# Sigmoid attention and an MLP mixer on one core: batch 0's u transposed by DMA, and each v loaded behind its transposed q

## The chip, the cores and the metric

The kernel runs on one core of one Trainium2 chip. The metric is the device time of one execution, in microseconds (us), on that core. The engines are named as in the profile: PE (TensorE, matrix products; PEld its weight loads), DVE (VectorE), ACT (ScalarE), POOL (GpSimd) and SP (SyncE, which here only issues DMAs). All engines run beside each other, each through its own instructions in order, and wait for one another by semaphores. DMAs are issued by SP, POOL or ACT, queue by queue, and are carried out by the core's 16 DMA engines.

## The reference

For each of 8 batches and 12 heads (448 positions, head width 64), attention with a sigmoid in place of a softmax; then, for each batch, an MLP mixer on the result x of 448 x 768.

```
scores = q @ k.T / 8 - log(448)          per head
attn   = sigmoid(scores) ;  x_head = attn @ v
x      = heads side by side              [448, 768]
h      = relu(x.T @ w_tok1) @ w_tok2     token mixing, 448 -> 256 -> 448
u      = x + h.T
out    = u + relu(u @ w_ch1) @ w_ch2     channel mixing, 768 -> 1536 -> 768
```

Inputs and output are fp32; the kernel computes in fp16 with fp32 accumulation.

## The kernel before

**Stage 1** goes through 24 units, three for each batch b: unit (b, u) holds four heads, and cycle c = 3b + u of the main loop (L566) works on it. Each unit needs q and k with the head width on the partitions ("transposed", tiles tr_q and tr_k). `qk` (L146) multiplies them in seven blocks j, and ACT takes the sigmoid (L161). `av` (L171), in the cycle behind, multiplies by v (tile raw_v) and DVE copies the result to xT (L190). x is transposed by SP's DMA (`xtrans_dma`, L200) or by PE (`xtrans`), `tok1` (L222) and `ytrans` (L249) do the token mixing, and DVE adds x to give `ut`, u with the channels on the partitions (L261).

**Stage 2** of a batch (`stage2`, L450) is the channel mixing: `ch1` (L279) in 12 column blocks of 72 products, each block copied through a relu by DVE (L294), then `ch2` (L301) for three tiles of 128 rows in two halves, and `ch2_last` (L342) for the last 64 rows. It is cut into pieces of three products, and `work` (L580) puts these between the qk blocks of the cycles after, by shares of the whole: batch 0's in cycles 4 to 7, later ones over three cycles. Batch 0 does its first halves first, since the second half of the weight c2 is loaded later (L427).

**The last addition, out = u + ...**, needs u with the positions on the partitions. Here the kernel knows two ways. From batch 1 on, `utrans` (L266) lets SP transpose the whole of `ut` by one DMA into the tile `un`, and DVE adds `un` to ch2's PSUM result (L319, L379). Where `un` does not exist, PE adds u in PSUM by products with an identity matrix (L327 for ch2, L365 for ch2_last), and DVE only copies (L334, L377). Before the change batch 0 goes the second way; so does the last tile of the last batch. Both are in the two functions:

```
    add_on_pe = final or b not in un
...
        if b in un:
            nc.vector.tensor_tensor(
                out=outs[b, t][:, cols].rearrange("s (u d) -> s u d", d=128),
                in0=un[b][:, NU * half : NU * half + NU, t, :],
                in1=ps[:, 0:DH].rearrange("s (u d) -> s u d", d=128),
                op=ADD,
            )
```

PSUM tiles of all these steps share the tag "m" with four buffers; qk's have two of their own.

**Loads and queues.** POOL issues all loads in the order of the program (`load`, L87: two DMAs, one for each half of the partitions, which also turn fp32 into fp16). Weights and batches 0 to 2 are loaded at the start. Batch 0 and some units of batches 1 and 2 are transposed by PE (`pe_transpose`, L132). The others, from batch 2's second unit on, go `through_dma` (L121): DVE regroups a unit's k or q (`relayout`, L103), and SP transposes (`dma_transpose`, L116) all units of k, then of q. These pieces are put between the pieces of stage 2 by `work`: batch 2's in cycle 5, batch 3's in cycles 7 and 8, and those of batch b + 1 from cycle 3b on.

At the end of cycle (b, 2) POOL copies two elements of the next batch's last transposed q into the tile `gate` (L632). It reads what the DMA transpose wrote, so POOL waits there, and the loads of k and q for batch b + 2 come after. The load of v for batch b + 1 stands elsewhere: in cycle (b, 0), b > 1, behind the third qk block (L599). raw_v has two buffers.

SP's queue has, in order, the transposes of x, of k and q, of u (`utrans(b - 1)` in cycle (b, 2), b > 1) and the output's stores.

Of the kernel before, what the change touches and what calls it, by code (L numbers as in the profile page):

```python
# [22 lines left out]
NU = 3  # L23
# [3 lines left out]
def kernel(  # L27
# [13 lines left out]
    B, H, S, E = q.shape  # L41
# [35 lines left out]
    def raw_tile(b, t):  # L77
        if (b, t) not in raw:
            tag, bufs = f"raw_{t}", 2 if t == "v" else 1
            if b == 1 and t != "v":  # L80
                tag = f"rel_{t}"
            raw[b, t] = pa.tile(
                [128, NU, 2, NJ, E], FP16, tag=tag, bufs=bufs, name=f"raw_{t}_{b}"
            )
        return raw[b, t]

    def load(b, t, src, u0, u1):  # L87

        for g in range(2):
            dst = raw_tile(b, t)[64 * g : 64 * g + 64, u0:u1, :, :, :]  # L90
            heads = src[b, 6 * g + 2 * u0 : 6 * g + 2 * u1]
            nc.gpsimd.dma_start(  # L92
                out=dst.rearrange("p u hi j e -> p (u hi) (j e)"),
                in_=heads.rearrange("h (p j) e -> p h (j e)", j=NJ),
            )
# [25 lines left out]
    def through_dma(b, u0):  # L121

        pieces = []
        for t in ("k", "q"):
            for u in range(u0, NU):
                pieces.append(lambda t=t, u=u: relayout(b, t, u))
            pieces.append(lambda t=t: dma_transpose(b, t, u0))
        return pieces
# [17 lines left out]
    def qk(b, u, j):  # L146
        if j == 0:
            att[b, u] = pa.tile(
                [128, 2, NJ, S], FP16, tag="att", bufs=2, name=f"att_{b}_{u}"
            )  # L150
        ps = pp.tile([128, 2, 512], FP32, tag="qk", bufs=2, name=f"qk_{b}_{u}_{j}")
        for g in range(2):
            for hi in range(2):
                nc.tensor.matmul(  # L154
                    out=ps[64 * g : 64 * g + 64, hi, 0:S],
                    lhsT=tr[b, "k"][64 * hi : 64 * hi + 64, u, j, 64 * g : 64 * g + 64],
                    rhs=tr[b, "q"][64 * hi : 64 * hi + 64, u, :, 64 * g : 64 * g + 64],
                    start=True,
                    stop=True,
                )  # L160
        nc.scalar.activation(  # L161
            out=att[b, u][:, :, j, :],
            in_=ps[:, :, 0:S],
            func=SIGMOID,
            bias=bias_t[:, :],
            scale=att_scale,
        )
# [3 lines left out]
    def av(b, u, j0=0, j1=NJ):  # L171
        if j0 == 0:
            xa[b, u] = [
                pp.tile([128, 512], FP32, tag="m", bufs=4, name=f"xa_{b}_{u}_{g}")
                for g in range(2)
            ]
        ps = xa[b, u]
        for j in range(j0, j1):
            for g in range(2):
                for hi in range(2):  # L180
                    nc.tensor.matmul(  # L181
                        out=ps[g][64 * hi : 64 * hi + 64, 0:S],
                        lhsT=raw[b, "v"][64 * g : 64 * g + 64, u, hi, j, :],
                        rhs=att[b, u][64 * g : 64 * g + 64, hi, j, :],
                        start=(j == 0),
                        stop=(j == NJ - 1),
                    )
        if j1 == NJ:
            for g in range(2):
                nc.vector.tensor_copy(  # L190
                    out=xTs[b % 2][:, u, g, 0:S], in_=ps[g][:, 0:S]
                )
# [7 lines left out]
    def xtrans_dma(b, u):  # L200
        nc.sync.dma_start_transpose(
            out=xn_tile(b)[:, u, :, :, :].rearrange("s g t d -> s (g t) d"),
            in_=xTs[b % 2][:, u, :, :].rearrange("d g s -> d (g s)"),
        )
# [61 lines left out]
    def utrans(b):  # L266
        un[b] = pa.tile([128, NDB, 4, 128], FP16, tag="un", bufs=2, name=f"un_{b}")
        nc.sync.dma_start_transpose(
            out=un[b].rearrange("s db t d -> s (db t) d"),
            in_=uts[b % 2].rearrange("d db s -> d (db s)"),  # L270
        )
# [7 lines left out]
    def ch1(b, cb, d0=0, d1=NDB):  # L279
        if cb == 0 and d0 == 0:  # L280
            h2[b] = pa.tile([128, NCB, S], FP16, tag="h2", bufs=1, name=f"h2_{b}")
        if d0 == 0:
            acc[b, cb] = pp.tile([128, 512], FP32, tag="m", bufs=4, name=f"c1_{b}_{cb}")
        ps = acc[b, cb]
        for d in range(d0, d1):
            nc.tensor.matmul(  # L286
                out=ps[:, 0:S],
                lhsT=c1[:, BY_UNIT[d], 128 * cb : 128 * cb + 128],
                rhs=uts[b % 2][:, BY_UNIT[d], 0:S],
                start=(d == 0),  # L290
                stop=(d == NDB - 1),
            )
        if d1 == NDB:
            nc.vector.tensor_scalar(  # L294
                out=h2[b][:, cb, :], in0=ps[:, 0:S], scalar1=0.0, scalar2=None, op0=MAX
            )
# [153 lines left out]
    def stage2(b):  # L450
        for cb in range(NCB):
            for d in range(0, NDB, 3):
                yield 3 * S, lambda cb=cb, d=d: ch1(b, cb, d, d + 3)
        groups = [(t, half) for t in range(3) for half in range(2)]
        if b == 0:
            groups.sort(key=lambda g: g[1])
        for t, half in groups:
            for n in range(0, NCB, 3):
                yield 3 * DH, lambda t=t, half=half, n=n: ch2(b, t, half, n, n + 3)
        for n in range(0, NCB, 3):  # L460
            yield 3 * DH, lambda n=n: ch2_last(b, n, n + 3)
# [97 lines left out]
    for cb in range(2):  # L559
        ch1(0, cb, 5, 6)  # L560

    ON_DMA = range(N_FIRST, N_CYCLES)
    ON_PE = 2 * NU + 1
    starts = [N_FIRST] + [NU * b + 5 for b in range(1, B - 1)] + [N_CYCLES + 1]
    pending, copies = [], []
    for c in range(N_FIRST, N_CYCLES + 1):  # L566
        b, u = divmod(c, NU)
        here = c < N_CYCLES
        before = divmod(c - 1, NU)
        mixed = [n for n in (c - 2, c - 1) if (n == c - 1) != (n in ON_DMA) or not here]  # L570
        if c in starts:
            lot = starts.index(c)
            first = c
            pending = list(stage2(lot))[4 if c == N_FIRST else 0 :]
            total = sum(w for w, f in pending)

            shares = [9, 9, 6, 6] if c == N_FIRST else [10, 10, 10]
            spent = [0, 0]

        def work(share):  # L580
            goal = 3 * sum(shares[: c - first]) + share * shares[c - first]
            while pending and spent[0] < total * goal / 90:
                w, f = pending.pop(0)
                f()
                spent[0] += w
                spent[1] += 1
                if copies and (c < 3 * NU or spent[1] % 2 == 0):
                    copies.pop(0)()

        if here:  # L590
            qk(b, u, 0)
            qk(b, u, 1)
        av(*before)
        if c - 1 in ON_DMA:
            xtrans_dma(*before)
        if here:
            qk(b, u, 2)
        if here and b > 1 and u == 0 and b + 1 < B:
            load(b + 1, "v", v, 0, NU)  # L599
        if c == 2 * NU + 2:  # L600
            copies += through_dma(3, 0)[NU + 1 :]
        work(1)
        if c - 1 not in ON_DMA:
            xtrans(*before)
        if c + 1 < ON_PE:
            for t in ("k", "q"):
                pe_transpose(*(divmod(c + 1, NU)[0], t, divmod(c + 1, NU)[1]))
        if here:
            qk(b, u, 3)
            qk(b, u, 4)  # L610
        if b == 1 and u == 2:
            copies = through_dma(2, 1)
        if c == 2 * NU + 1:
            copies = through_dma(3, 0)[: NU + 1]
        work(2)
        if u == 2 and b > 1:
            utrans(b - 1)
        for n in mixed:
            tok1(*divmod(n, NU))
        if here:  # L620
            qk(b, u, 5)
            qk(b, u, 6)
        if b > 2 and u == 0 and b + 1 < B:
            copies = through_dma(b + 1, 0)
        work(3)
        for n in mixed:
            ytrans(*divmod(n, NU))
        if b == 1 and u == 2:
            while copies:
                copies.pop(0)()  # L630
        if here and u == 2 and b + 2 < B:
            nc.gpsimd.tensor_copy(  # L632
                out=gate[:, :], in_=tr[b + 1, "q"][:, NU - 1, NJ - 1, 126:128]
            )
            load(b + 2, "k", k, 0, NU)
            load(b + 2, "q", q, 0, NU)
    assert not copies
    utrans(B - 1)
    for w, f in pending:
# [33 lines left out]
```

## Time and profile before

| | us |
|---|---|
| median of 3 runs | 370.6 (370.51 to 370.81) |
| the profiled execution | 370.7 |
| its span in the trace | 368.9 |
| L286, ch1's 576 products, busy | 115.5 |
| L309, ch2's 576 products, busy | 100.4 |
| L161, the 168 sigmoids, busy | 158.8 |
| L327 and L365, identity products, busy | 2.0 (18) and 0.7 (12) |
| un<-ut, 7 transposes, median to landing | 7.4 |
| raw_v, 12 whole loads of a half, median to landing | 9.8 |

A line of the profile's groups or timeline names the line of the kernel, the engine, the operation, and out<-in by the program's tile names ("c" is any tile of ch1, ch2 or their weights). The timeline gives start and duration in us; matmuls are pipelined, so neighbours overlap, and the time that one takes from PE is read from the start of the next. "To landing" runs from the issue to the semaphore of the finished DMA. In the DMA view q0 is the queue of POOL's loads and q1 that of SP's transposes and stores; a packet of a transpose is 256 bytes. In the 40 slices of the span a digit is the busy share in tenths.

### The profile page before, as it was taken

What the parts mean: (1) busy time and instruction counts of PE and PEld (TensorE: products, weight loads), DVE (VectorE), ACT (ScalarE), POOL (GpSimd) and SP (SyncE); (2) the same over time, 40 slices, a digit from 0 to 9 for tenths busy, and PEclk for the clock granted to TensorE, in tenths of its full rate; (3) what the DMA queues carried; (4) which work ended last, traced back from release to release, by engine and by line L of the source; (5) the groups of instructions that cost most, each with busy time, mean ns of one, the idle gap of its engine ahead of it and who ended that gap; (6) DMA issues with size and microseconds to landing.
All of it is one profiled execution on the core that took longest, in us unless ns stands there. A gap on an engine that the chain in (4) does not pass through costs nothing.

```text
span 368.9 us, 7559 instructions
## 1 busy us (share of the span) xinstructions
PE 361.3 (98%) x3272; PEld 196.8 (53%) x3272; DVE 181.8 (49%) x322; ACT 172.2 (47%) x212; POOL 53.0 (14%) x91
## 2 busy tenths in 40 slices
PE   8989999999999999999999999999999999999995
PEld 5545555555555555555545555555545554565553
DVE  2466657257445365364455464554552354644531
ACT  1996555665445455455445545454454554010000
POOL 8847410120030031001110030100000000000000
PEclk9999999999999999999999999999999999999999
DMA  7999999999999998769996899939910425137014
GB/s 95 176 202 190 197 205 196 140 193 226 212 171 172 204 186 156 99 129 204 177 148 85 150 188 148 170 75 176 195 22 11 112 71 110 28 78 158 2 43 107
DMA packets 103872, 51.73 MB, mean 140 GB/s; under 512 B 76000, under 2 KB 100768, under 8 KB 103840
## 3 DMA queue, kind: packets, MB, share of 16 engines
q1 hardware_dynamic: 78736, 29.47, 43.9%
q0 software_dynamic: 25024, 21.70, 39.2%
q8 instruction: 25, 0.41, 0.5%
q10 hardware_dynamic: 80, 0.10, 0.1%
q14 instruction: 7, 0.06, 0.0%
HBM read 43.38 MB, written 11.01 MB: 147 GB/s over the span
## 4 chain that ended last, share of the span: by engine, by line
PE 95%; DVE 2%; ACT 2%; issue 0%
PE c L286 30%; PE c L309 26%; PE qk L154 10%; PE xa L181 9%; PE tk L233 6%; PE yt L254 5%; PE c L354 5%; ACT att L161 2%; PE heat L469 2%; DVE xT L190 1%; PE tp_k L138 1%; PE tp_q L138 0%; DVE xn L215 0%; PE c L327 0%; DVE h L243 0%; PE xb L210 0%
## 5 line engine op out<-in xcount | busy, mean ns | idle before, releaser
L161 ACT ACTIVATE att<-qk,att_bias 128x896 f16<-128x896 f32 x168 | 158.8, 1010 | 101.7 <-PE qk L154 101.4
L286 PE MATMUL c<-ut,c 128*128 128x448 f16 x576 | 115.5, 353 | 0.0
L309 PE MATMUL c<-c,h 128*128 128x384 f16 x576 | 100.4, 326 | 0.0
L294 DVE TENSOR_SCALAR h<-c 128x448 f16<-128x448 f32 x96 | 59.8, 624 | 60.6 <-PE c L286 60.4
L286 PEld LDWEIGHTS <-c 128*128 128x128 f16 x576 | 53.3, 98 | 58.7 <-issue 13.0
L309 PEld LDWEIGHTS <-h 128*128 128x128 f16 x576 | 54.1, 98 | 42.9 <-issue 9.1
L154 PE MATMUL qk<-tr_q,tr_k 64*64 64x448 f16 x672 | 53.3, 361 | 1.1 <-ACT att L161 1.0
L319 DVE TENSOR_TENSOR o<-un,c 128x384 f32<-128x384 f16 x42 | 23.3, 554 | 62.2 <-PE c L309 62.1
L190 DVE CAST xT<-xa 128x448 f16<-128x448 f32 x48 | 27.7, 620 | 20.8 <-PE xa L181 20.8
L181 PE MATMUL xa<-att,raw_v 64*64 64x448 f16 x672 | 37.6, 350 | 0.0
L247 ACT ACTIVATE h<-tk 128x256 f16<-128x256 f32 x42 | 13.8, 380 | 49.9 <-PE tk L233 49.9
L261 DVE TENSOR_TENSOR ut<-xT,yt 128x448 f16<-128x448 f16 x48 | 27.4, 615 | 4.6 <-PE yt L254 4.4
L154 PEld LDWEIGHTS <-tr_k 64*64 64x64 f16 x672 | 15.9, 104 | 25.1 <-issue 21.7
L181 PEld LDWEIGHTS <-raw_v 64*64 64x64 f16 x672 | 22.6, 107 | 10.1 <-issue 1.3
L233 PE MATMUL tk<-xn,w 128*128 128x256 f16 x192 | 25.0, 272 | 1.3 <-DVE xn L215 0.9
L233 PEld LDWEIGHTS <-w 128*128 128x128 f16 x192 | 18.6, 98 | 7.0 <-issue 2.6
L254 PE MATMUL yt<-w,h 128*128 128x448 f16 x96 | 22.2, 353 | 0.0
L375 ACT ACTIVATE o<-c 64x384 f32<-64x384 f32 x1 | 0.5, 485 | 40.5 <-PE c L365 40.5
L632 POOL COPY gate<-tr_q 128x2 f16<-128x2 f16 x5 | 0.9, 184 | 125.2 <-DMA tr_q<-rel_q 125.2
L92 POOL DMA_DIRECT2D raw_v<-in_v_dram x20 | 13.0, 669 | 36.1 <-PE qk L154 35.9
L92 POOL DMA_DIRECT2D raw_q<-in_q_dram x26 | 16.6, 653 | 8.4 <-DMA c<-in_moe_w_ch_dram 5.0
L92 POOL DMA_DIRECT2D raw_k<-in_k_dram x26 | 16.4, 649 | 8.6 <-DMA c<-in_moe_w_ch_dram 5.2
(42 smaller groups left out, 128.4 us busy)
## 6 DMA issues: line engine op xcount, KB each, us to landing
out_dram<-o SPq DMA_DIRECT2D x48, 192.0 KB, 2.8
c<-in_moe_w_ch_dram POOLq DMA_DIRECT2D x4, 1152.0 KB, 14.3
raw_v<-in_v_dram POOLq DMA_DIRECT2D x12, 336.0 KB, 9.8
raw_k<-in_k_dram POOLq DMA_DIRECT2D x10, 336.0 KB, 6.1
raw_q<-in_q_dram POOLq DMA_DIRECT2D x10, 336.0 KB, 9.5
raw_q<-in_q_dram POOLq DMA_DIRECT2D x14, 112.0 KB, 5.6
raw_k<-in_k_dram POOLq DMA_DIRECT2D x14, 112.0 KB, 4.5
out_dram<-o SPq DMA_DIRECT2D x15, 96.0 KB, 2.3
```

What stands on the lines that cost most here:

```text
L92: nc.gpsimd.dma_start(out=dst.rearrange("p u hi j e -> p (u hi) (j e)"), in_=heads.rearrange("h (p j) e -> p h (j e)", j=NJ),)
L154: nc.tensor.matmul(out=ps[64 * g : 64 * g + 64, hi, 0:S], lhsT=tr[b, "k"][64 * hi : 64 * hi + 64, u, j, 64 * g : 64 * g + 64], rhs=tr[b, " ...
L161: nc.scalar.activation(out=att[b, u][:, :, j, :], in_=ps[:, :, 0:S], func=SIGMOID, bias=bias_t[:, :], scale=att_scale,)
L181: nc.tensor.matmul(out=ps[g][64 * hi : 64 * hi + 64, 0:S], lhsT=raw[b, "v"][64 * g : 64 * g + 64, u, hi, j, :], rhs=att[b, u][64 * g : 64 ...
L190: nc.vector.tensor_copy(out=xTs[b % 2][:, u, g, 0:S], in_=ps[g][:, 0:S])
L233: nc.tensor.matmul(out=ps[:, tcb, :, :], lhsT=w1[:, t, cols], rhs=xn[b][:, u, :, t, :], start=(t == 0), stop=(t == 3),)
L254: nc.tensor.matmul(out=ps[:, 0:S], lhsT=h1[b][:, tcb, g, u, :], rhs=w2[:, tcb, :, :], start=(tcb == 0), stop=(tcb == 1),)
L261: nc.vector.tensor_tensor(out=uts[b % 2][:, db, 0:S], in0=xTs[b % 2][:, u, g, 0:S], in1=ps[:, 0:S], op=ADD)
L286: nc.tensor.matmul(out=ps[:, 0:S], lhsT=c1[:, BY_UNIT[d], 128 * cb : 128 * cb + 128], rhs=uts[b % 2][:, BY_UNIT[d], 0:S], start=(d == 0), ...
L294: nc.vector.tensor_scalar(out=h2[b][:, cb, :], in0=ps[:, 0:S], scalar1=0.0, scalar2=None, op0=MAX)
L309: nc.tensor.matmul(out=ps[:, 0:DH], lhsT=h2[b][:, cb, 128 * t : 128 * t + 128], rhs=c2[:, cb, cols], start=(cb == 0), stop=(cb == NCB - 1 ...
L319: nc.vector.tensor_tensor(out=outs[b, t][:, cols].rearrange("s (u d) -> s u d", d=128), in0=un[b][:, NU * half : NU * half + NU, t, :], in ...
```

## The change

`utrans(0)` is called before the main loop, behind the first pieces of batch 0's ch1. So `un[0]` exists when batch 0's stage 2 is written out: its identity products are not issued, and DVE adds `un[0]` in place of its copies. And the load of v for batch b + 1 (b > 1) moves from cycle (b, 0) to the end of cycle (b, 2), behind the gate and ahead of the loads of k and q. A sixth gate is added in cycle (6, 2), for the v of batch 7. The v of batches 0 to 2 stays where it was.

```diff
     for cb in range(2):
         ch1(0, cb, 5, 6)
 
+    utrans(0)
     ON_DMA = range(N_FIRST, N_CYCLES)
...
         if here:
             qk(b, u, 2)
-        if here and b > 1 and u == 0 and b + 1 < B:
-            load(b + 1, "v", v, 0, NU)
         if c == 2 * NU + 2:
             copies += through_dma(3, 0)[NU + 1 :]
...
-        if here and u == 2 and b + 2 < B:
+        if here and u == 2 and b + 1 < B:
             nc.gpsimd.tensor_copy(
                 out=gate[:, :], in_=tr[b + 1, "q"][:, NU - 1, NJ - 1, 126:128]
             )
-            load(b + 2, "k", k, 0, NU)
-            load(b + 2, "q", q, 0, NU)
+            if b > 1:
+                load(b + 1, "v", v, 0, NU)
+            for t, src in (("k", k), ("q", q)):
+                if b + 2 < B:
+                    load(b + 2, t, src, 0, NU)
```

## The prediction

> **What bounds the kernel now.** I read the page's busy rows and the chain first, then PE's timeline around batch 0's second stage, then the DMA queues there, one microsecond at a time.
>
> ```profile
> PE 361.3 (98%) x3272; PEld 196.8 (53%) x3272; DVE 181.8 (49%) x322; ACT 172.2 (47%) x212; POOL 53.0 (14%) x91
> PE   8989999999999999999999999999999999999995
> DMA  7999999999999998769996899939910425137014
> PE 95%; DVE 2%; ACT 2%; issue 0%
> ```
>
> TensorE works for 98% of the span and is 95% of the chain. Work taken from it shortens the run; anything else counts only if PE has to wait for it. The DMA row is full up to the fifteenth slice (about 138 us), so from 38 to 138 us an added transfer delays those behind it. The clock row is 9 throughout.
>
> All working is on the profiled execution: 370.7 us, span 368.9, so 1.8 around the span. The median shown, 370.6, is 0.1 lower.
>
> **What is removed: batch 0's identity products.** PE's timeline, columns start and duration (durations overlap, so I take differences of starts):
>
> ```profile
> 62.80 0.66 PE L309 MATMUL c<-c,h 128*128 128x384 f16 x3
> 63.30 0.33 PE L327 MATMUL c<-ident,ut 128*128 128x128 f16 x3
> 63.46 2.11 PE L309 MATMUL c<-c,h 128*128 128x384 f16 x12
> ...
> 84.10 1.65 PE L354 MATMUL c<-c,h 128*64 128x384 f16 x18
> 85.59 0.33 PE L365 MATMUL c<-ident,ut 128*64 128x128 f16 x6
> 85.86 0.93 PE L254 MATMUL yt<-w,h 128*128 128x448 f16 x4
> ```
>
> Three L327 products take 63.46 - 63.30 = 0.16 us. There are six such groups (they start at 63.30, 65.41, 70.26, 73.86, 79.03 and 81.75): 0.98. The six L365 products take 85.86 - 85.59 = 0.27, of which about 0.08 stays, since batch 1's L354 group also ends 0.08 late (24 products in 2.07 us at 0.083): 0.19. Sum 1.17, call it **1.2 us saved**. The upper bound is 1.45, if the 0.26 between L327 and the next matmul of another shape (65.41 to 65.67, 81.75 to 82.01) and all 0.27 go. VectorE pays nothing: six copies of 558 ns (L334) become six adds of 554 (L319), two of 554 (L377) become two of 552 (L379).
>
> **What is added: one transpose of u, 24 blocks of 128 rows, 3072 packets of 256 B, on SP's queue.** Batch 0's last u add ends at 38.2 on DVE, and SP has issued nothing by then (its first line is at 56.91), so the issue itself delays nothing. The packets do. One-microsecond slices of the DMA queues (packets, MB, share), at 59, 61 and 70 us; q0 carries POOL's loads, q1 SP's transposes:
>
> ```profile
> q0 software_dynamic: 260, 0.20, 130.2%
> ```
> ```profile
> q0 software_dynamic: 170, 0.15, 89.2%
> q1 hardware_dynamic: 168, 0.04, 32.1%
> ```
> ```profile
> q1 hardware_dynamic: 1143, 0.28, 127.2%
> ```
>
> Alone, the loads move 260 packets per us and a transpose 1143. Together each gets about 170, packet for packet: the transpose drops to a seventh, the loads lose a quarter. (The same in 109 to 114 us: 166 to 179 each.)
>
> Now step by step. A transpose issued among loads shows its first packets 4 to 4.7 us later (56.91 to about 60.9; 103.94 to 108.6), so this one starts at 42.6. The slices from there to 67 us hold 5280 load packets, of which 3070 are of c2 (smaller: 266 per us alone, so about 185 beside a transpose). 3070 / 185 + 2210 / 172 = 29.4 us: loads that ended at about 65 to 67 now end near 72. Beside them q1 goes at about 177 per us:
> - u of batch 0: 3072 / 177 = 17.4, ends at 60, lands at 61 to 62. First needed by the add after 63.3. In time; late, it would hold PE only from about 67.4, when the four PSUM tiles "m" are used up.
> - The second half of c2 landed at 62.8 (issue 44.78 + 18.0). Its data ended at about 60.5, 17.9 us after 42.6; at the shared rate these become 25.3, so it lands at 70.2. First needed by the fourth L309 group, at 70.43 less three groups of 0.16: 69.9. **Late by 0.3.**
> - v of batch 2 landed at 66.7, now about 73.5; needed by L181 at 76.26 less 0.65. In time.
> - Behind u on SP:
>
> ```profile
> 56.91 1.34 SPq L201 DMA_TRANSPOSE xn<-xT  x1
> 62.18 4.16 SPq L116 DMA_TRANSPOSE tr_k<-rel_k  x1
> 66.39 2.99 SPq L116 DMA_TRANSPOSE tr_q<-rel_q  x1
> 69.42 1.31 SPq L201 DMA_TRANSPOSE xn<-xT  x1
> ```
>
> That is 1024 packets of xn, 1792 of tr_k, 1792 of tr_q. xn ends at 42.6 + 4096 / 177 = 65.7, lands near 67.5, needed at 71.89 - 0.5: in time. The q of batch 2 lands at 71.4 now (66.39 + 5.0). With u ahead, 7680 packets must pass. About 5000 have passed by 72; 2680 at 1143 take 2.3 us; the last packet to landing took 0.9: 75.2. SP's issue is held too: un<-ut (L268) took 8.9 us to issue at 177.97, with about 1600 packets outstanding at its end, so tr_q can't be issued freely: 75.5. Its user:
>
> ```profile
> 75.86 0.57 PE L154 MATMUL qk<-tr_q,tr_k 64*64 64x448 f16 x8
> ```
>
> This qk comes at 75.86 - 0.65 (four groups gone) = 75.2. **Late by 0.3**, the same 0.3 as c2's, not another: PE that waited for c2 comes here 0.3 later. I cost the transpose at **+0.3 us**. The ends: at 190 of each per us and a start at 42.1, q lands at 72.4 and costs 0; at 160, below any slice, loads end at 75.6, q lands at 78.6 and costs 3.4.
>
> [...]
>
> What comes after is later as well, but covered. The gate on POOL waits for that q (71.45, now near 76), so k of batch 3 lands at about 83 in place of 78.8, and its regrouping on DVE (79.87, then about 79.0) waits some 3.5 us. Behind it on DVE are the adds at 82.12 and 85.97, whose PSUM tiles PE needs again only at 86 to 87; DVE catches up in the 1.6 and 2.2 us that it idles there. Without that cover up to 2 us would come through.
>
> **What is moved: each v from batch 3 on.** v of batch 3 leaves 75.0, where it ran beside tr_k (issued 83.92 for 7.46 us, landing 10.9), so the next q transpose and its gate come earlier: DVE's regrouping ends at 91.9, hence the gate at about 96 to 98 in place of 100.12. POOL there:
>
> ```profile
> 100.12 0.18 POOL L632 COPY gate<-tr_q 128x2 f16<-128x2 f16 x1 [23.75 <-DMA tr_q<-rel_q]
> 100.72 1.32 POOL L92 DMA_DIRECT2D raw_k<-in_k_dram  x2 [0.41 <-issue]
> 102.96 1.33 POOL L92 DMA_DIRECT2D raw_q<-in_q_dram  x2 [0.92 <-issue]
> 104.26 1.34 POOL L92 DMA_DIRECT2D raw_v<-in_v_dram  x2
> ```
>
> k lands at 107.5 and 109.3, q at 111.6 and 113.8, v at 116.2 and 117.6. In the new order v takes k's place, and lands at about 109 if the gate stays, 105 if it comes early; the first L181 of batch 3 is at 115.79 - 1.2 = 114.6. Covered by 5 us or more. k takes q's place: 113.8, or about 109.5 with the early gate; its regrouping (L103) is at 110.63 - 1.2 = 109.4. DVE's next add waits 2.35 us for PE now, which takes up most of a delay. I cost it at 0; without the cover, up to 2.
>
> The other batches have more room. The gates open at 130.3, 173.1 and 216.1, and a new one for batch 7 at 252.95 + 6.7 = 259.7; add 9 to 14 for v's landing; the first L181 is at 158.4, 201.1, 243.7 and 286.4: 12 us or more each. Queued on POOL behind each gate are v, k and q only, and k and q, some 5 us later, are first used some 20 us after their gate. The u transposes issued there (133.95, 177.97, 219.30) now share with six loads in place of four, 3 to 4 us longer; the tightest, 219.30, landed 14.9 later at 234.2, now about 238, for an add at 238.05 - 1.2, and the four PSUM tiles cover about 4 us of that. Zero.
>
> **Sum:** 370.7 - 1.2 + 0.3 = 369.8 on the profiled execution, 0.1 less on the median: **369.7 us**, 0.24% faster. 0.2% (0.74 us) is about the least that a measurement of this kernel can tell from no change.
>
> **The rivals.**
> 1. *The gain is given back* (c2's second half, or batch 2's transposed q, 0.5 to 1.9 us late at 69.9 or 75.2). For it: both come out within 0.3 us of their need, and my estimates of landings are good to about 1 us. Against: u's transpose starts among loads of large packets and may go more slowly, and the loads then lose less. One us of stall gives 370.5.
> 2. *Slower: the q of batch 2 becomes the bound.* The place is the qk at 75.2; the mechanism is SP's queue, where 3072 packets now stand before xn, tr_k and tr_q, and q1 gets a seventh of its speed until the loads are out. It decides from a landing 1.9 us late, that is at 77.1 or later. By the bound of 160 packets it lands at 78.6: 370.6 - 1.2 + 3.4 = 372.8. For it: the tail after the loads is slow now too (296 to 548 q1 packets per us from 65 to 68). Against: xn between u and tr_k has long passed by then, and POOL issues no load until the q has landed, so at the end q1 is alone.
> 3. *v or k behind the gate is late.* v would have to land after 114.6, 14 us after a gate at 100; behind k and q it took 12.7 at most (issue 104.9), so only a gate later than about 101 brings it there. For it: the delay of rival 2 pushes the whole of batch 3's chain. Against: the chain loses v's 768 packets, 3.3 us of load time, ahead of it. A k or v that costs 2 us beyond its cover gives 369.7 + 2 = 371.7.
> 4. *No stall at all*, the bound of 190: 370.6 - 1.2 = 369.4, at most 1.45 saved, 369.15.
>
> **How the numbers follow.** The forecast and rival 4, at most 0.45 us of stall: 0.46 (0.20 of it rival 4). Rival 1: 0.27. Rival 2: 0.20. Rival 3: 0.07. Faster by over 0.2% means below 369.86: the first two, 0.46. Within 0.2%, up to 371.34: rival 1, 0.27. Slower: rivals 2 and 3, 0.27. The range goes from rival 4 with a little of the larger saving (369.2) to near the bound of rival 2 (372.4), so that most of both signs is in; some 0.15 is left out. The forecast's own range is 369.2 to 369.9.
>
> **What would show it.** L327 and batch 0's L365 are gone, and L319 has 48 adds. The new un<-ut is issued at 38.3, takes over 10 us to issue, and lands at 60 to 63. In 43 to 60 us q1 shows some 170 to 185 packets per us, the loads 0.13 to 0.15 MB. PE runs 0.5 us ahead at the fourth L309 group, then meets a wait of some 0.3 us on c2 or on tr_q at 75. After 87 it is ahead by a constant 0.9 and has no new waits up to the end. The second L632 starts at 96 to 98, and v lands before L181 asks for it. I am wrong if the lead grows or shrinks after 90, if L319 of batch 0 is held by un, or if q1 gets another share beside the loads than one packet for one.

## The result, and the profile after

The changed kernel takes **375.03 us** (median of 6 runs, 373.78 to 376.13); the kernel before took 370.89 on the same chip (6 runs, 370.51 to 372.0). The ratio is 1.0105, with a 95% interval of 1.0085 to 1.0125: about 1.1% slower, where 0.24% faster was forecast. The time lies above the upper end of the range, 372.4. The profiled execution took 375.4 us, with a span of 373.6: 4.7 longer than before's 368.9.

The page of the changed kernel: busy row of the engines, 40 slices of PE, of its granted clock and of the DMA engines, the chain, and the group of ch2's products.

```profile
PE 361.0 (97%) x3248; PEld 194.8 (52%) x3248; DVE 181.8 (49%) x322; ACT 172.6 (46%) x212; POOL 53.3 (14%) x92
...
PE   7989999799999999999999999999999999999995
...
PEclk9999999899999999999999999999999999999999
DMA  7999999999999899939996799919961426127014
...
PE 72%; DMA 20%; POOL 4%; DVE 2%; issue 1%; DVEq 0%; POOLq 0%
...
L309 PE MATMUL c<-c,h 128*128 128x384 f16 x576 | 101.3, 329 | 2.6 <-DMA c<-in_moe_w_ch_dram 2.6
```

PE has 24 instructions fewer (3248 against 3272), as the change intends, but its busy time hardly fell. Both the PE row and the clock row dip in the eighth slice, 65 to 75 us, and 20% of the chain now goes through a DMA. The L309 group's idle time before its products, 2.6 us, is put down to one thing: the load of the weight c2. (The chain's shares are coarse: once a DMA is on the way back, the chain follows everything that this DMA waited for.)

PE's timeline at that place and at the two later waits; the last column in brackets is the idle time before the line and what ended it:

```profile
69.66 0.66 PE L309 MATMUL c<-c,h 128*128 128x384 f16 x3
72.95 2.98 PE L309 MATMUL c<-c,h 128*128 128x384 f16 x9 [2.62 <-DMA c<-in_moe_w_ch_dram]
75.77 1.04 PE L233 MATMUL tk<-xn,w 128*128 128x256 f16 x8
...
79.56 0.57 PE L154 MATMUL qk<-tr_q,tr_k 64*64 64x448 f16 x8
...
90.93 1.51 PE L181 MATMUL xa<-att,raw_v 64*64 64x448 f16 x26 [0.26 <-DVE o L379]
...
120.56 1.51 PE L181 MATMUL xa<-att,raw_v 64*64 64x448 f16 x26 [0.82 <-DVE ut L261]
```

Before, at the same place:

```profile
70.43 1.63 PE L309 MATMUL c<-c,h 128*128 128x384 f16 x9
71.89 1.04 PE L233 MATMUL tk<-xn,w 128*128 128x256 f16 x8
```

The nine L309 products began at 70.43 and the next group, L233, at 71.89: 1.46 us for nine. Now they begin at 72.95, and L233 at 75.77: 2.82 for the same nine. So PE loses twice here: it stands, from about 70.15 (0.5 after 69.66) to 72.95, and then works at half its speed. The windows view (length, busy time and instructions by engine, then the granted clock, the DMA share and GB/s) has both:

```profile
70.00:73.00 3.00, 0.38 (x3) 0.06 (x2) 0.55 (x1) 1.50 (x2) 0.00 (x0) 0.88 1.25 193
73.00:76.00 3.00, 3.00 (x12) 1.50 (x13) 0.00 (x0) 0.00 (x0) 0.00 (x0) 0.55 1.28 192
76.00:79.00 3.00, 3.00 (x27) 1.71 (x25) 0.56 (x1) 2.16 (x4) 0.00 (x0) 1.00 1.32 210
```

The windows are 70 to 73, 73 to 76 and 76 to 79 us. The granted clock is 0.55 in the second. Cut finer, it is 1.00 up to 72.31, 0.50 from there to 75.72, and 1.00 after that:

```profile
72.31:75.72 3.41, 2.77 (x9) 1.35 (x10) 0.00 (x0) 0.00 (x0) 0.00 (x0) 0.50 1.24 195
```

So it fell 0.6 us before the wait ended. Before, it was 1.00 in all three windows; the one with the nine products:

```profile
70.00:73.00 3.00, 3.00 (x27) 2.01 (x29) 0.56 (x1) 1.63 (x3) 0.77 (x2) 1.00 0.82 170
```

**A ledger of PE's schedule**, each term a difference of the same starts in the two traces, before and after (qk at 72.86 and 76.73, at 75.86 and 79.56, at 86.72 and 89.92, at 88.44 and 92.10, at 115.21 and 118.98, at 116.95 and 121.72):

| | us |
|---|---|
| identity products gone | -1.2 |
| standing for c2's second half | +2.8 |
| nine products at half clock | +1.4 |
| DVE held by batch 3's k, PE waits at 90.9 | +0.5 |
| DVE held by batch 4's k, PE waits at 120.6 | +1.0 |
| up to 66 us and small rests | +0.2 |
| sum (373.6 - 368.9) | +4.7 |

SP's queue in the stretch, issue times and how long the issue took:

```profile
38.47 11.60 SPq L268 DMA_TRANSPOSE un<-ut  x1
57.14 1.77 SPq L201 DMA_TRANSPOSE xn<-xT  x1
63.21 6.39 SPq L116 DMA_TRANSPOSE tr_k<-rel_k  x1
69.65 7.54 SPq L116 DMA_TRANSPOSE tr_q<-rel_q  x1
```

u lands 24.7 after its issue, at 63.2. Nothing waits for it. The q of batch 2 lands 9.6 after its issue, at 79.2; since PE comes to its qk at 79.56 after all the rest, it adds nothing either. What is late is the load that u's packets ran beside.

**Where c2 lost its time.** One-microsecond slices of the DMA queues of the changed kernel, at 51, 45 and 69 us (packets, MB, share; q0 the loads, q1 the transposes):

```profile
q0 software_dynamic: 186, 0.14, 90.7%
q1 hardware_dynamic: 185, 0.05, 35.8%
```
```profile
q0 software_dynamic: 43, 0.03, 24.6%
q1 hardware_dynamic: 33, 0.01, 12.2%
```
```profile
q0 software_dynamic: 55, 0.04, 91.8%
q1 hardware_dynamic: 52, 0.01, 77.5%
```

The first slice is as forecast: packet for packet, 185 of each. The others were not in the forecast: both queues nearly stop. There are four such gaps before c2 has landed, at 44.6 to 45.9, 57.0 to 57.9, 59.4 to 59.9 and 69.2 to 69.9. Counted in half-microseconds against 185 per us, the loads lost 188, 141, 78 and 130 packets in them, 537 in all, or 2.9 us. The second half of c2 landed at 72.9 (issued 47.07, 25.8 later); the forecast was 70.2.

Each gap follows, by 1 to 2 us, the transfer of an instruction block, at 43.5, 55.5, 58.0 and 68.0. In the slice at 43 us it is the third line:

```profile
q0 software_dynamic: 173, 0.14, 91.1%
q1 hardware_dynamic: 154, 0.04, 33.6%
q8 instruction: 1, 0.02, 8.8%
```

Further gaps follow the blocks at 112.5, 140.0, 187.5 and 229.5, by less than 1 to more than 2 us (in their lowest half microsecond 4, 28, 28 and 13 packets of loads and 3, 37, 37 and 13 of transposes). The first of these, 113.0 to 114.4, lies inside the load of batch 4's k (issued 105.43, awaited until 117.84). By the packets missing from its slices beside 170 per us, it cost that load some 1.4 us (an estimate), so it has a part in the +1.0 of the ledger. The kernel before has instruction blocks at 43.8, 55.1 and 56.9 us, where only loads run, and no gap follows: each half microsecond up to 61 has 117 to 136 packets. After its block at 67.1, where only transposes run, q1 goes from 530 packets in the half microsecond at 67.0 to 18, 14 and 128 in the next three, and back to 586 at 69.0, while tr_k, issued at 62.18, lands only at 70.0: a gap without loads. The same is in the changed kernel after a block at 95.0, where q1 runs alone: 565 packets in that half microsecond, then 465, 7, 18 and 266. One stretch of the kernel before, 223 to 226, is low (75, 120 and 140 load packets per us) some 4 us after a block at 218.9; whether it is such a gap is not shown.

### The profile page after: what moved, and what is told of

Same layout as the page of the kernel before. It is cut to its first block, busy times and chain, and to the rows that moved or that the text cites. A ratio compares the mean times of both kernels' runs of the same rounds, so it can differ in the third digit from the quotient of the medians.

```text
span 373.6 us, 7516 instructions
## 1 busy us (share of the span) xinstructions
PE 361.0 (97%) x3248; PEld 194.8 (52%) x3248; DVE 181.8 (49%) x322; ACT 172.6 (46%) x212; POOL 53.3 (14%) x92
## 4 chain that ended last, share of the span: by engine, by line
PE 72%; DMA 20%; POOL 4%; DVE 2%; issue 1%; DVEq 0%; POOLq 0%
PE c L286 25%; PE c L309 22%; DMA c<-in_moe_w_ch_dram 10%; PE qk L154 7%; PE xa L181 6%; DMA raw_k<-in_k_dram 5%; PE tk L233 4%; PE c L354 4%; PE yt L254 4%; DMA raw_q<-in_q_dram 4%; POOL raw_k L92 2%; DMA w<-in_moe_w_tok_dram 2%; POOL raw_q L92 1%; POOL raw_v L92 1%; DVE rel_k L103 1%
## 5 line engine op out<-in xcount | busy, mean ns | idle before, releaser
L309 PE MATMUL c<-c,h 128*128 128x384 f16 x576 | 101.3, 329 | 2.6 <-DMA c<-in_moe_w_ch_dram 2.6
L294 DVE TENSOR_SCALAR h<-c 128x448 f16<-128x448 f32 x96 | 59.9, 625 | 60.2 <-PE c L286 59.9
L309 PEld LDWEIGHTS <-h 128*128 128x128 f16 x576 | 54.5, 98 | 47.0 <-issue 10.3
L319 DVE TENSOR_TENSOR o<-un,c 128x384 f32<-128x384 f16 x48 | 26.6, 554 | 68.9 <-PE c L309 65.4
L233 PE MATMUL tk<-xn,w 128*128 128x256 f16 x192 | 25.0, 272 | 1.3 <-DVE xn L215 0.9
L233 PEld LDWEIGHTS <-w 128*128 128x128 f16 x192 | 18.6, 98 | 7.2 <-issue 2.7
L354 PE MATMUL c<-c,h 128*64 128x384 f16 x192 | 17.3, 328 | 0.0
```

Source lines behind the costliest of these rows:

```text
L233: nc.tensor.matmul(out=ps[:, tcb, :, :], lhsT=w1[:, t, cols], rhs=xn[b][:, u, :, t, :], start=(t == 0), stop=(t == 3),)
L294: nc.vector.tensor_scalar(out=h2[b][:, cb, :], in0=ps[:, 0:S], scalar1=0.0, scalar2=None, op0=MAX)
L309: nc.tensor.matmul(out=ps[:, 0:DH], lhsT=h2[b][:, cb, 128 * t : 128 * t + 128], rhs=c2[:, cb, cols], start=(cb == 0), stop=(cb == NCB - 1 ...
L354: nc.tensor.matmul(out=ps[g], lhsT=h2[b][:, n, 384:448], rhs=c2[:, n, DH * g : DH * g + DH], start=(n == 0), stop=(n == NCB - 1 and not ad ...
```

## The experiments

All kernels below are **stand-ins**: each DMA transpose of SP is replaced by a plain DMA of the same bytes in rows of 256 bytes, the size of a transpose's packet. They leave the transposition by DMA out. The destination tiles get rows 136 elements apart, and the packets have about 256 bytes (s_after, 36 to 50 us: 1353 packets, 0.35 MB on q1):

```diff
-        nc.sync.dma_start_transpose(
-            out=un[b].rearrange("s db t d -> s (db t) d"),
-            in_=uts[b % 2].rearrange("d db s -> d (db s)"),
+        nc.sync.dma_start(
+            out=un[b][:, :, :, 0:128].rearrange("s db t d -> s (db t) d"),
+            in_=uts[b % 2].rearrange("d db (t s) -> d (db t) s", t=4),
         )
```

The order of the program, the packets' number and size and the waits stay. So the stand-ins test the forecast's own picture, in which a transpose is 256-byte packets in a queue and nothing else; where they differ from the real kernel, something about transposes is missing from that picture. My theory after the result was that the transpose of u alone makes the loss, through c2, by the number of its packets, as the forecast had it, with an error of size. Its rivals were that the moved v makes it, and that it comes from the transposing itself and not from rows in a queue. With real transposes only the kernels before and after were measured. The runs below come from three chips, on which the kernel before took 370.74, 370.91 and 371.14; each ratio is to the kernel before on the same chip.

**The kernel before and the changed one as stand-ins.** s_before is the edit above alone, s_after has the whole change too.

> A stand-in of the kernel before: each of SP's DMA transposes is a plain copy of the same bytes on the same queue, in rows of 256 bytes (the destination tiles are padded so that rows don't merge). The transposition by DMA is left out, so later values are of other elements; all instructions and sizes stay. If a transpose loads the queues like so many rows of 256 bytes, it takes 370 to 371.5 us, and beside loads q1 and q0 move row for row, some 170 to 190 per us each. If transposes have a cost of their own, the copies land earlier and the time is the same or less, since PE is the bound.

> The stand-in of the changed kernel, made in the same way (the transposition by DMA is left out). My theory (u's 3072 rows share the queues with c2's load, row for row): c2's second half lands at 70 us or later, PE waits for it, and the time is 1 to 5 us above the stand-in of before. If the loss comes from the transposing itself and not from rows in the queue: 1.2 us below the stand-in of before.

Measured: s_before 370.57 (ratio to the kernel before 0.9996, interval 0.9987 to 1.0006), so the stand-in serves as a base. s_after 370.48 (0.9986, interval 0.9969 to 1.0003). **The 4.1 us of loss are gone**, though every packet of u is still there. So my theory missed (1 to 5 us above s_before): the number of packets alone does not make the loss. Its c2 landed at 67.0 and PE stood for it nowhere. Its slice at 57 us, with an instruction block in it:

```profile
q0 software_dynamic: 175, 0.14, 88.4%
q1 hardware_dynamic: 175, 0.04, 34.3%
q14 instruction: 1, 0.01, 1.9%
```

The blocks come at 43.5, 55.5, 57.0 and 67.5, within 1 us of the changed kernel's, beside loads and rows of 256 bytes, and no gap follows any of them. So the gaps come with transposes; plain rows in their place do not make them. That a gap also takes an instruction block is argued from the times alone; loads it does not take, as the one at 67.5 in the kernel before shows. The two kernels differ in more than the gaps: in s_after q1 is nearly idle from 59.5 to 61, and POOL's earlier load of c2 (L429) is issued at 34.18 in place of 35.48, before any packet of u moves. So this does not show that the gaps are the whole of c2's 5.9 us.

The 1.2 us saved do not show in s_after's time either. Its span is 368.7 against 368.8. One wait of PE took most of it:

```profile
87.06 1.51 PE L181 MATMUL xa<-att,raw_v 64*64 64x448 f16 x26 [0.73 <-DVE o L379]
```

DVE had waited 4.7 us for the k of batch 3, which the later gate (75.05; 70.95 in s_before) lets in later; the add at L379 stands behind that regrouping and frees the PSUM tile that PE needs. The forecast had named this chain and costed it at nothing.

**Each part alone.** s_u adds only `utrans(0)` to s_before, s_v only moves the loads of v.

```diff
+    utrans(0)
```
```diff
-        if here and b > 1 and u == 0 and b + 1 < B:
-            load(b + 1, "v", v, 0, NU)
...
+            if b > 1:
+                load(b + 1, "v", v, 0, NU)
```

> The stand-in of before with utrans(0) alone; every load of v at its old place (the transposition by DMA is left out). My theory: this half makes nearly all of the loss, so within 1 us of the changed stand-in, above the stand-in of before. The rival (the moved v makes the loss, since k stands behind it and DVE waits for k): 1 us below the stand-in of before.

> The stand-in of before with the moved loads of v alone, identity products kept (the transposition by DMA is left out). My theory: the gate opens as before, k of batch 4 lands behind v, DVE's wait for it costs PE at most 0.8 us: from 0.3 below to 0.9 above the stand-in of before. The rival (the moved v makes the loss): 3 us or more above it.

Measured: s_u 372.48 (1.0045, interval 1.0027 to 1.0063), s_v 370.53 (0.9989, interval 0.9979 to 1.0). The moved v alone does nothing; the transposed u alone costs 1.9 against s_before; with the moved v the sum is -0.1. The expectation for s_v was met; s_u, 2.0 above s_after, met neither of its two. **So among the stand-ins the moved v makes no loss; s_after, with it, is 2.0 us below s_u.** In the changed kernel itself the first moved load of v is issued at 104.14, when the 2.8 and 1.4 us at c2 are long lost. PE's new waits in s_u:

```profile
75.95 0.57 PE L154 MATMUL qk<-tr_q,tr_k 64*64 64x448 f16 x8 [0.75 <-DMA tr_q<-rel_q]
...
87.39 1.51 PE L181 MATMUL xa<-att,raw_v 64*64 64x448 f16 x26 [0.33 <-DVE o L379]
...
102.31 0.57 PE L154 MATMUL qk<-tr_q,tr_k 64*64 64x448 f16 x8 [1.18 <-DMA tr_q<-rel_q]
```

The first is the tight point that the forecast had at 75.2 with a wait of 0.3: it is there, 0.75 long, with the gate at 75.87 (the forecast said near 76). The third is the same queue one batch on. In s_after, with v behind the gate, both are gone. For the third the reason is that batch 3's chain has 768 packets less ahead of it. The first can't be v's doing, since up to that gate both kernels issue the same transfers; s_k3_later below, with v moved too, has it again, 0.24 long. It is a point with no slack that some executions miss.

**The saving alone.** s_no_dma gives `un[0]` as a view of `uts[0]`: the identity products go, and no DMA comes.

```diff
+    un[0] = uts[0].rearrange("p db (t d) -> p db t d", d=128)
```

> The stand-in of before without batch 0's identity products and without a copy in their place: DVE adds batch 0's u as it lies (the transposition of batch 0's u is left out too; the rest as in the stand-in). If the products are worth the 1.2 us of the forecast: 369.4 against the stand-in's 370.6, ratio about 0.9968. If PE's time for them is hidden: 370.4 to 370.8.

Measured: 369.45 (0.9956, interval 0.9944 to 0.9968), 1.1 below s_before; span 367.6, 1.2 below. The saving is as forecast.

**Standing for c2, made on purpose.** s_late is s_after with one more load, 896 rows of a weight into a tile that nobody reads, ahead of c2's second half. s_late_filled also gives PE 26 idle products, whose result nobody reads, before the group that waits.

```diff
+    junk = pc.tile([128, 7, DH], FP16, name="junk")
+    nc.gpsimd.dma_start(
+        out=junk[:, :, :],
+        in_=moe_w_ch2.rearrange("(cb c) d -> c cb d", cb=NCB)[:, 0:7, 0:DH],
+    )
     load_c2(1)
```
```diff
+                if (b, t, half, n) == (0, 0, 1, 0):
+                    yield 3 * DH, lambda: (new_heat(), keep_warm(26), ch2(0, 0, 1, 0, 3))
+                    continue
```

> The stand-in of the changed kernel with one more load on POOL, 896 rows of w_ch2 into a tile that nothing reads, just ahead of c2's second half. It takes the place of the some 3 us in which the queues stood still in the changed kernel's trace, so that c2's second half lands near 72 to 73 us in place of 67. My theory (c2's lateness and what follows from it are the loss): PE waits 2 to 4 us at the fourth L309 group, its products after that run at about half speed for some 3 us, and the time is 374 to 377. The rival (in the changed kernel the transposes themselves slow PE or cost later on): no more than the wait, 372 to 373.5, with full-speed products after it.

> The same with 26 idle products on a constant tile (26 x 0.107 = 2.8 us) just ahead of the fourth L309 group, where PE waits for c2. If the slow products after the wait come from the granted clock that falls when PE stands still, they run at full speed here, and the time is about 1.5 us below the one without idle products. If they are slow for another reason (weights still arriving), it is the same or above.

Measured: s_late 375.77 (1.0106, interval 1.0074 to 1.0138), s_late_filled 375.11 (1.011, interval 1.0084 to 1.0135). With four runs each and 3 us between the lowest and the highest, the times do not tell the two apart. The traces do. First s_late, PE's line and the windows 70 to 73, 73 to 76 and 76 to 79:

```profile
75.52 3.06 PE L309 MATMUL c<-c,h 128*128 128x384 f16 x9 [5.68 <-DMA c<-in_moe_w_ch_dram]
```
```profile
70.00:73.00 3.00, 0.00 (x0) 0.00 (x0) 0.43 (x1) 1.02 (x2) 0.00 (x0) 0.92 1.26 192
73.00:76.00 3.00, 0.48 (x2) 0.28 (x3) 0.00 (x0) 0.00 (x0) 0.00 (x0) 0.50 1.24 194
76.00:79.00 3.00, 3.00 (x12) 1.51 (x10) 0.00 (x0) 0.00 (x0) 0.00 (x0) 0.50 1.27 236
```

Then s_late_filled, the same place and windows:

```profile
69.62 3.00 PE L477 MATMUL heat<-warm 128*128 128x256 f16 x26
75.05 1.64 PE L309 MATMUL c<-c,h 128*128 128x384 f16 x9 [2.43 <-DMA c<-in_moe_w_ch_dram]
```
```profile
70.00:73.00 3.00, 2.62 (x24) 2.10 (x22) 0.37 (x1) 0.96 (x2) 0.00 (x0) 1.00 1.26 192
73.00:76.00 3.00, 0.95 (x6) 0.60 (x7) 0.00 (x0) 0.00 (x0) 0.00 (x0) 1.00 1.24 200
76.00:79.00 3.00, 3.00 (x28) 1.74 (x26) 0.30 (x1) 1.40 (x3) 0.00 (x0) 1.00 1.13 223
```

c2 comes at about the same time, but with 3 us of idle products in its way PE stands 2.43 us only, the clock stays at 1.00, and the nine products take 1.64 in place of 3.06: 1.4 us, the term of the ledger. By the windows' means (0.92 and 0.50 above, 0.95 in 79 to 82) the half clock of s_late lasts from about 72.5 to 79.3 and slows the next group too; s_late_filled has a wait of its own further on, 0.70 at 81.09 for the q of batch 2. The profiled spans differ by 1.5 (375.1 and 373.6). So the half clock comes from PE's standing, not from the transposes: there are none in these kernels.

**The same on the kernel before's stand-in**, with two such loads of 1024 rows (s_c2_late), and with the idle products too (s_c2_late_filled).

```diff
+    junk = pc.tile([128, 8, DH], FP16, name="junk")
+    for _ in range(2):
+        nc.gpsimd.dma_start(
+            out=junk[:, :, :],
+            in_=moe_w_ch2.rearrange("(cb c) d -> c cb d", cb=NCB)[:, 0:8, 0:DH],
+        )
     load_c2(1)
```

> The stand-in of before (identity products, no u of batch 0 on the queue; transposition by DMA left out) with two more loads on POOL ahead of c2's second half, 1024 rows of w_ch2 each into a tile that nothing reads, so that c2 alone comes late, at about 72 us or later. PE's wait at the fourth L309 group is W, read from the trace. If standing still also lowers the granted clock, the nine products after the wait take about 3.0 us in place of 1.5, the clock reads 0.5 to 0.6 there, and the time is the stand-in's 370.6 + W + 1.5. If a wait costs only itself: 370.6 + W.

> The same with 26 idle products on a constant tile (2.8 us) ahead of the fourth L309 group. If the clock is the cause of the slow products, it stays at 1.0 here, they take 1.5 us, and the time is about 1.5 us below the one without idle products. If not, the time is the same or above.

Measured: 380.44 (1.0263, interval 1.0231 to 1.0295) and 380.11 (1.0242, interval 1.0213 to 1.0271). Both expectations missed the time. In s_c2_late the nine products began at 75.96 in place of 70.33 (s_before), 5.6 late, and took 3.06 at a clock of 0.50. But the half clock did not end with them: by the windows' means (0.83 in 73 to 76, 0.50 in 76 to 79, 0.53 in 79 to 82) it lasted from about 75.0 to 81.8. The L309 group at 73.26 in s_before starts at 81.55 here, 8.3 late, so the half clock cost 2.7 us where 1.5 was expected, and with 0.3 further on the span is 377.4 in place of 368.8. (The profiled execution took 379.1, the shortest of five; what makes the median 1.3 longer is not known.) In s_c2_late_filled 3 us of idle products were too short for the delay:

```profile
76.47 1.83 PE L309 MATMUL c<-c,h 128*128 128x384 f16 x9 [3.25 <-DMA c<-in_moe_w_ch_dram]
```
```profile
76.00:79.00 3.00, 2.53 (x14) 1.58 (x15) 0.00 (x0) 0.00 (x0) 0.00 (x0) 0.79 1.24 193
79.00:82.00 3.00, 3.00 (x22) 1.33 (x21) 0.14 (x1) 1.95 (x4) 0.00 (x0) 0.64 1.26 239
```

After 3.25 us of standing the clock falls all the same, by the windows' means (0.79 and 0.64) from about 77.8 to 81.2, when PE has been at work again for 1.3 us.

**The wait on k, moved away.** s_k3_later is s_after with the regrouping of batch 3's k one piece of `work` later in its cycle, so that DVE's adds come ahead of it.

```diff
-        if c == 2 * NU + 1:
-            copies = through_dma(3, 0)[: NU + 1]
         work(2)
...
+        if c == 2 * NU + 1:
+            copies = through_dma(3, 0)[: NU + 1]
         work(3)
```

> The stand-in of the changed kernel with the regrouping of batch 3's k moved from the second to the third share of cycle 7, behind the ch2 add that it held up (the trace shows DVE waiting 4.7 us for that k, and PE then 0.7 us for DVE at L181). If that wait is what eats the saved 1.2 us: 369.6 to 369.9, ratio 0.997 to 0.998. If something else does: 370.3 to 370.7, as the stand-in of the changed kernel.

Measured: 371.04 (1.0, interval 0.998 to 1.002), not below s_after's 370.48. The wait at 87 is gone, but PE now waits 0.24 for batch 2's q at 75.44 and 0.47 behind DVE's ut at 115.50. The wait moved, and the expectation missed.

**Half of the transpose.** s_half is s_after with only the second halves of batch 0's u by DMA: 1536 packets in place of 3072, and the identity products of the first halves stay. s_half_u is the same with v's loads at their old place.

```diff
     def utrans(b):
+        lo = NU if b == 0 else 0
...
-            out=un[b][:, :, :, 0:128].rearrange("s db t d -> s (db t) d"),
-            in_=uts[b % 2].rearrange("d db (t s) -> d (db t) s", t=4),
+            out=un[b][:, lo:NDB, :, 0:128].rearrange("s db t d -> s (db t) d"),
+            in_=uts[b % 2][:, lo:NDB, :].rearrange("d db (t s) -> d (db t) s", t=4),
...
+    def by_dma(b, half):
+        return b in un and (b > 0 or half == 1)
```

> The stand-in of the changed kernel with only the second halves of batch 0's u (1536 of 3072 rows) copied by DMA and added by DVE; the first halves keep their identity products (transposition by DMA left out). By my sum 0.6 us of PE's work goes, the queue is lengthened by 2.5 us in place of 5, batch 2's transposed q lands at about 73.5, before its user at 75.5, and k of batch 3 comes early enough to spare PE's wait for DVE: 369.9 to 370.2. If a smaller u on the queue does not spare the waits: 370.4 or more.

> The same half of u, with every load of v at its old place. If the moved v helps only by making room behind a late gate, and the gate is hardly late here: within 0.3 us of the one with the moved v. If the old place costs as much as beside the whole u (2.0 us between the two stand-ins): 371.5 to 372.2.

Measured: s_half **370.01** (0.9973, interval 0.9961 to 0.9984), 0.56 below s_before, which is about half of the 1.2 (by the ratios to the kernel before on each chip, 0.9973 and 0.9996, it is 0.85); PE has no wait in it that s_before does not have, and the first gate is at 72.96 in place of 75.05. s_half_u 371.10 (0.9991, interval 0.9975 to 1.0007), with waits of 0.39 at 87.08 (DVE's o) and 0.98 at 101.79 (batch 3's q). Neither of the two expectations for s_half_u was met. So v's move is worth 1.1 us beside half of u, 2.0 beside the whole, and nothing without. s_half is faster than the kernel before, as a stand-in; with real transposes it was not tried.

## Why the prediction was wrong

**Right.** PE sets the time (busy for 361.0 of the 373.6 us), and the identity products are worth 1.2 us (s_no_dma). A transpose among loads gets one packet for one; 185 of each was measured, 185 forecast beside c2's packets. u's own landing, 63.2 (forecast 61 to 62), bounds nothing. The two tight points were the right ones: c2 at 69.9 and the q of batch 2 at 75.2; the latter is the first wait of s_u. v lands in time everywhere.

**Wrong: "I cost the transpose at +0.3 us".** This is the term that failed, in three parts.

1. *"Late by 0.3"* for c2's second half. It was 2.8. The slices were extrapolated from stretches of the kernel before in which loads and transposes run together but no instruction block comes (61 to 63 and 109 to 114 us), so that no gap was in them. By count the four gaps are as large as the miss (2.9 us of packets, 2.7 of landing), and in the stand-ins, without transposes, no gap follows the blocks. The agreement is in part luck: the stand-ins, which are the forecast's own picture, landed c2 at 67.0 (s_after) and 68.6 (s_u), earlier than its 70.2, and 4.3 to 5.9 before the changed kernel's 72.9. So the picture was 1.6 to 3.2 us too slow elsewhere, and what besides the gaps made c2 late is not shown. Why a gap occurs stays open: it would take kernels with other DMA transposes, which were not tried.
2. *No price for what standing does to the clock.* The sum let a wait cost its own length. A wait of 2.8 us cost 1.4 more, since the nine products after it ran at a clock of 0.50. s_late and s_late_filled show this term without transposes.
3. *"What comes after is later as well, but covered"*. The gate came at 79.35, not near 76, and the covers that I had named were too thin: DVE waited 4.2 us for batch 3's k, and 3.4 for batch 4's, which v's loads now precede and which has a gap in it.

```profile
79.35 0.19 POOL L631 COPY gate<-tr_q 128x2 f16<-128x2 f16 x1 [29.91 <-DMA tr_q<-rel_q]
80.30 1.31 POOL L92 DMA_DIRECT2D raw_k<-in_k_dram  x2 [0.76 <-PE qk L154]
...
103.68 0.19 POOL L631 COPY gate<-tr_q 128x2 f16<-128x2 f16 x1 [20.75 <-DMA tr_q<-rel_q]
104.14 1.32 POOL L92 DMA_DIRECT2D raw_v<-in_v_dram  x2 [0.27 <-PE c L286]
105.43 1.34 POOL L92 DMA_DIRECT2D raw_k<-in_k_dram  x2
```
```profile
87.70 0.62 DVE L103 COPY rel_k<-raw_k 128x896 f16<-128x896 f16 x1 [4.22 <-DMA raw_k<-in_k_dram]
...
117.84 0.62 DVE L103 COPY rel_k<-raw_k 128x896 f16<-128x896 f16 x1 [3.36 <-DMA raw_k<-in_k_dram]
```

The same wait at 0.73 us in s_after, where c2 is in time, shows that this part was wrong for itself: even with the gate at 75.05 the cover was some 0.7 short. The second gate, forecast at 96 to 98, came at 103.68; in s_after it came at 98.31.

**The rivals.** Rival 1 named c2's second half among what could give the gain back, but ended at 1.9 us of stall. Rival 2 had the sign, slower, and a stall not far from the right size, 3.4 beside 2.8; but it put the bound at the q of batch 2, and the trace has it at c2: the packets ahead of q were the smaller trouble. Rival 3 occurred in part: batch 4's k, behind v and with a gap in its load, cost 1.0. No rival joined them, and the range ended at the price of one.

Outside the gaps, u's transpose was as fast beside loads as a plain DMA of the same packets: at 51 us it moved 185 packets in a microsecond, 0.05 MB, and the plain rows of s_after moved 185 and 0.05 MB in the same slice. In the stretches compared, the gaps came with transposes only.

## What to carry to other kernels

Work that goes from a saturated engine to a DMA queue can be paid for by whoever shares the queue: here 1.2 us left PE, u's own landing held nothing, and the load of c2 beside it landed at 72.9 in place of 62.8. So look for the transfer beside it with the least slack, not for its own landing. Measure that slack against a wait's whole price: here its length (2.8), the half-speed products behind it (1.4) and the waits that came later (0.5 and 1.0). When a full transfer overruns the slack, half of it can still pay (as stand-ins, 0.9973 of the kernel before with half of u, 0.9986 with the whole), so size the transfer by the slack.

## What was not expected of the hardware

- Two DMA queues that nearly stop for 0.5 to 1.3 us (33 to 55 packets of each in the microseconds at 45, 57 and 69 in place of 185; 39 and 28 in the half microsecond at 59.5), within 1 to 2 us after each of the four instruction blocks from 43 to 68 us, where transposes and loads run together. In the kernel before q1 does so with transposes alone, after the block at 67.1: 18, 14 and 128 packets in the half microseconds from 67.5 to 69.0, with 530 ahead of them and 586 behind. With plain rows in place of transposes none follows the blocks of the same stretch in s_after (77 or more load packets in each half microsecond from 43 to 69.5), and none shows in the slices taken of s_u and s_late (169 or more of each at 45, 57 and 69 us). That the blocks cause them is not shown.
- A granted clock of 0.50 for 3.41 us (the changed kernel, from 72.31) and, by the windows' means, for about 3.4 (s_c2_late_filled, from 77.8) and 6.8 (s_late, from 72.5; s_c2_late, from 75.0), around waits of 2.62, 3.25, 5.68 and 5.37 us, and none around a wait of 2.43 (s_late_filled). The length of the wait does not decide it alone: the changed kernel's clock fell when PE had stood 2.0 us (70.33 to 72.31), less than the 2.43 that went without a fall, and in s_c2_late_filled it fell after the wait. In each of the four, PE had been idle for about 2.0 us or more of the 3.41 us ahead of the fall, but in s_late_filled for 2.43 us of such a stretch without a fall. What decides it is not shown.
- The issue of a DMA transpose among loads kept SP for 11.6 us (u, 38.47), that of the plain stand-in for 0.7. What follows on SP's queue comes after that: the changed kernel's tr_q is issued at 69.65, when the 6.39 us of tr_k's issue at 63.21 are over. It is not a matter of transposes alone: the plain tr_q of s_after (63.21) kept SP for 5.1 us.
